# Another order of the 8 KB blocks of keys and values over the partitions

## The chip, the core and the metric

The kernel runs on one core of one Trainium2 chip. The time is device microseconds of one execution. The core has five engines: TensorE (PE, matrix products), VectorE (DVE), ScalarE (ACT), GpSimd (POOL) and SyncE (SP). Each has its own instruction stream, and they wait for one another with semaphores. On-chip memory (SBUF) has 128 partitions. Transfers between HBM and SBUF are carried by 16 DMA engines of the core; an instruction on SP's queue only starts a transfer.

## The reference

The program is the forward and backward pass of one decoding step: an attention block with cached keys and values beside a gated product of three weight matrices, both on a layer-normed row of 576 numbers, for a batch of 2. The gradients of all inputs but B_x are outputs, those of the caches too.

```python
q = (x @ wq).reshape(B, Sq, Hq, Dh).transpose(0, 2, 1, 3)   # 32 heads of 128, Sq = 1
k = jnp.repeat(k_cache, rep, axis=1)                        # 16 key heads, rep = 2
v = jnp.repeat(v_cache, rep, axis=1)
scores = jnp.einsum("bhqd,bhkd->bhqk", q, k) * (Dh ** -0.5) # 4096 keys
p = softmax(scores, axis=-1)
o = jnp.einsum("bhqk,bhkd->bhqd", p, v)
A = o.transpose(0, 2, 1, 3).reshape(B, Sq, Hq * Dh) @ wo
...
g = jnp.einsum("bsd,df->bsf", x, w_gate)
u = jnp.einsum("bsd,df->bsf", x, w_up)
Bo = jnp.einsum("bsf,fd->bsd", g * u, w_down)
...
return x + A + Bo                                           # and its vjp with grad_out
```

All data are bfloat16. One head of keys (or values) of one batch entry is 4096 rows of 128 numbers, 1 MiB. There are 32 such heads of keys and 32 of values, and 32 gradients of each kind to write.

## The kernel before

Everything is cut into 16 steps (s): a step is a group g of two key heads and one batch entry b. In a step two heads of keys and two of values are loaded, each into one tile `big` of 128 partitions x 4096 numbers. Partition p holds 32 keys in a row, the 8 KB block p of the 1 MiB. The keys are turned by VectorE (line 466, 32 x 32 blocks), scored against the queries on TensorE (`score`, line 1277), and go through a softmax over all keys of a head, in which maximum and sum run over partitions and free dimension alike. `dscore` does the same for values and the gradient of the output. `contract` (line 1451) sums values over keys with the weights, and keys over the score gradients, with the tiles as they were loaded. `head_outer` makes the gradient of one head of keys or values as an outer product (line 1299) into PSUM; ScalarE and VectorE copy it (lines 470 and 472) into another tile `big`, from which a store of 1 MiB writes it out. The same order of blocks holds in the loads, in all of the computation and in the stores.

Beside this run the weight matrices: their products with the rows, and their gradients, which are outer products too and are stored from tiles `big` and from two small tiles `tl` (the last 64 rows of a gradient, 64 KB).

The order of the instructions is settled before the launch. A planner (class `Order`) keeps a model of time, and generators yield what they want next: an engine for so long, a buffer, a wait, a transfer. It picks by start time and priority and so writes five fixed instruction streams. Nearly every transfer is started from SP: the loads of keys and values at line 1152 (`load_kv`), weights at lines 1171 to 1207 (`load_w`), and stores at line 699 (`put`). At most eight transfers of SP's queue are on the way at a time.

The names that matter below: `views` and `oviews` (lines 1140 and 1141) are the HBM arrays of the caches and of their gradients, cut so that an index of batch and head gives one head as partitions x numbers. `load_kv` takes `views`, and `head_outer` hands an item of `oviews` to `put` in line 1293. `tail_outer` stores the last 64 rows. For some of them, named by `few` (from `FEW_M` and `FEW_G`), it writes the HBM side with an outer dimension of 4, so that SBUF's 64 rows stand against 4 x 16 rows of HBM:

```python
dsts = [d.rearrange("(r q) f -> q r f", q=4) if k in few else d for k, d in enumerate(dsts)]
...
FEW_M, FEW_G = (NFS - 1,), range(3, NG)
```

With NFS = 9 and NG = 8, and `few=(0, 1) if i in FEW_M else (1,)` in the weight part, `few=(0,) if g in FEW_G else ()` in the attention part, these are 10 and 5 stores of 26.

Of the kernel before, what the change touches and what calls it, by code (L numbers as in the profile page):

```python
# [13 lines left out]
P = 128  # L14
# [340 lines left out]
def kernel(  # L355
# [781 lines left out]
    wS = [[None] * 2 for _ in range(NS)]  # L1137
    bE = [[Event() for _ in range(2)] for _ in range(NS)]
    bS = [[None] * 2 for _ in range(NS)]
    views = [A.rearrange("b h (p c) d -> b h p (c d)", p=P) for A in (A_k_cache, A_v_cache)]  # L1140
    oviews = [A.rearrange("b h (p c) d -> b h p (c d)", p=P) for A in (out_2, out_3)]

    def load_kv():
        n = 0
# [457 lines left out]
```

## Time and profile before

| | |
|---|---|
| median of 3 runs | 465.51 us (462.81 to 465.99) |
| the profiled execution's own time | 463.56 us |
| its span (first to last instruction) | 461.7 us |
| mean granted TensorE clock | 0.722 of full speed |
| bytes read from HBM, bytes written | 92.48 MB, 92.48 MB |

The page gives the busy time of each engine and its share of the span, then the span in 40 slices of 11.54 us: a digit is the busy share in tenths, and the row GB/s says what the DMA engines moved. A row of a DMA queue gives packets, megabytes and the time that the packets took, as a share of the time of all 16 DMA engines. The rows of DMA issues give what is moved, how many transfers and their size; SPq and ACTq are the queues that start them. The chain of waits is followed back from the last instruction: at each step to what released it. In rows of one source line, three numbers with slashes are the least, the median and the greatest time of an instruction in ns; for a DMA that is the time on the issuing queue, waiting included, not the transfer. DMA packets stand by size: "under 2 KB" includes those under 512 B, and so on.

### The profile page before, as it was taken

The page shows a single profiled execution, that of the slowest core. Times are in us where ns is not written, and L with a number is a line of the kernel's source. Part 1 is how long each engine was busy: PE and PEld are TensorE (multiplying, and loading weights), DVE is VectorE, ACT ScalarE, POOL GpSimd, SP SyncE. Part 2 cuts the span into 40 slices and gives each one's busy share as a digit, 9 for nine tenths or more (in the row PEclk, how much of TensorE's full clock was granted, in tenths as well). Part 3 has the DMA queues.
Part 4 walks back from the last instruction along what each step waited for, and adds up shares of the span by engine and source line. Part 5 has one row for each costly group of instructions (what it writes and reads, how often), then busy time and mean ns, then how long its engine had stood idle before and what let it go on. Part 6 is the DMA issues. An engine that isn't in the chain of part 4 may idle for free.

```text
span 461.7 us, 15711 instructions
## 1 busy us (share of the span) xinstructions
PE 365.6 (79%) x6750; PEld 210.9 (46%) x6750; DVE 365.9 (79%) x708; ACT 337.1 (73%) x516; POOL 143.1 (31%) x174
## 2 busy tenths in 40 slices
PE   1687879798987677897687787778988886887986
PEld 1444455556443343454455353544533543443453
DVE  8897888887789687869887688977867887877682
ACT  4268648778986596765857778858857997897873
POOL 0740044303407342560016251140344563053000
PEclk9969575966775677758975798956567685666855
DMA  8999999999999999999999999999999999999985
GB/s 316 414 410 421 412 426 397 416 416 387 357 424 424 407 424 410 422 419 413 411 405 419 418 421 420 424 412 412 409 422 425 415 422 424 422 389 393 423 310 202
DMA packets 40530, 185.97 MB, mean 403 GB/s; under 512 B 3460, under 2 KB 12172, under 8 KB 24076
## 3 DMA queue, kind: packets, MB, share of 16 engines
q1 hardware_dynamic: 40452, 184.96, 98.7%
q8 instruction: 53, 0.87, 0.7%
q14 instruction: 17, 0.14, 0.1%
q10 hardware_dynamic: 8, 0.00, 0.0%
HBM read 92.48 MB, written 92.48 MB: 401 GB/s over the span
## 4 chain that ended last, share of the span: by engine, by line
DMA 48%; PE 24%; DVE 14%; ACT 10%; issue 3%; POOL 1%; SPq 0%; ACTq 0%; DVEq 0%; POOLq 0%
DMA out_dram<-big 23%; DMA big<-in_A_v_cache_dram 15%; ACT big L470 8%; DVE big L466 7%; DMA big<-in_B_w_up_dram 6%; PE ps_o L1299 4%; PE ps_o L730 3%; PE ps_m L1277 3%; DMA big<-in_A_k_cache_dram 3%; PE ps_m L1451 3%; DVE big L472 2%; PE ps_m L895 1%; PE ps_m L681 1%; PE ps_o L767 1%; POOL BD L1265 1%
## 5 line engine op out<-in xcount | busy, mean ns | idle before, releaser
L470 ACT CAST big<-ps_o 128x1024 bf16<-128x1024 f32 (+2 forms) x309 | 278.8, 964 | 47.6 <-PE ps_o L1299 24.1
L466 DVE STREAM_TRANSPOSE big<-big 128x1024 f32<-128x1024 f32 x146 | 176.4, 1223 | 19.5 <-DMA big<-in_A_v_cache_dram 7.5
L1265 POOL TENSOR_TENSOR BD<-vr,mask 128x2048 bf16<-128x2048 bf16 x32 | 115.2, 3602 | 117.8 <-DVE vr L472 47.2
L472 DVE CAST big<-ps_o 128x1024 bf16<-128x1024 f32 (+1 forms) x69 | 73.3, 1064 | 17.4 <-PE ps_o L767 7.8
L1242 POOL COPY W<-rep 32x16 bf16<-32x16 bf16 x128 | 24.6, 192 | 116.5 <-DVE rep L1015 100.5
L1277 PE MATMUL ps_m<-big,W 128*32 128x128 bf16 x2048 | 58.1, 275 | 2.7 <-issue 1.0
L1277 PEld LDWEIGHTS <-W 128*32 128x32 bf16 x2048 | 46.2, 123 | 23.1 <-issue 21.8
L1299 PE MATMUL ps_o<-BD,dd 32*128 32x512 bf16 x256 | 46.6, 502 | 10.0 <-ACT big L470 7.8
L1299 PE MATMUL ps_o<-BD,pp 32*128 32x512 bf16 x256 | 44.5, 472 | 8.8 <-ACT big L470 7.0
L466 DVE STREAM_TRANSPOSE big<-ww 128x1152 f32<-128x1152 f32 (+1 forms) x25 | 33.0, 1319 | 4.1 <-DMA out_dram<-big 4.0
L1451 PE MATMUL ps_m<-big,pp 128*32 128x512 bf16 x256 | 28.9, 540 | 4.4 <-DVE pp L466 3.6
L1451 PE MATMUL ps_m<-big,dd 128*32 128x512 bf16 x256 | 28.5, 539 | 3.4 <-DVE dd L466 2.1
L1299 PEld LDWEIGHTS <-dd 32*128 32x128 bf16 x256 | 11.0, 98 | 26.9 <-issue 19.9
L1299 PEld LDWEIGHTS <-pp 32*128 32x128 bf16 x256 | 10.2, 96 | 28.7 <-issue 24.5
L767 PEld LDWEIGHTS <-xnr 32*128 32x128 bf16 x368 | 13.3, 116 | 14.6 <-issue 13.6
L767 PE MATMUL ps_o<-D,xnr 32*128 32x128 bf16 x256 | 14.0, 269 | 5.5 <-ACT big L470 3.8
L730 PE MATMUL ps_o<-dyr,R 32*32 32x288 bf16 x256 | 17.4, 391 | 1.2 <-ACT big L470 1.2
L1047 POOL COPY qr<-qd 128x256 bf16<-128x256 bf16 x8 | 3.2, 395 | 45.6 <-DVE qd L472 41.8
L730 PE MATMUL ps_o<-dyr,hb 32*32 32x288 bf16 x288 | 14.6, 313 | 2.2 <-ACT big L470 2.1
L1461 ACT ACTIVATE osb<-ps_m 128x512 bf16<-128x512 f32 x14 | 8.5, 604 | 9.9 <-PE ps_m L1451 9.9
L681 PE MATMUL ps_m<-big,wm 128*32 128x128 bf16 x416 | 13.1, 284 | 2.1 <-DVE cr L1403 1.2
L895 PE MATMUL ps_m<-big,Wdy 128*128 128x128 bf16 x162 | 14.0, 254 | 1.0 <-DVE oT L1471 0.6
(210 smaller groups left out, 487.4 us busy)
## 6 DMA issues: line engine op xcount, KB each, us to landing
out_dram<-big SPq DMA_DIRECT2D x74, 1024.0 KB
big<-in_A_k_cache_dram SPq DMA_DIRECT2D x32, 1024.0 KB
big<-in_A_v_cache_dram SPq DMA_DIRECT2D x32, 1024.0 KB
out_dram<-big SPq DMA_DIRECT2D x17, 576.0 KB
ww<-in_B_w_down_dram SPq DMA_DIRECT2D x9, 576.0 KB
ww<-in_A_wo_dram SPq DMA_DIRECT2D x8, 576.0 KB
ww<-in_A_wq_dram SPq DMA_DIRECT2D x8, 512.0 KB
big<-in_B_w_gate_dram SPq DMA_DIRECT2D x4, 1024.0 KB
```

The lines of the kernel that those rows point to most:

```text
L466: nc.vector.transpose(out, in_)
L470: nc.scalar.copy(out, in_)
L472: nc.vector.tensor_copy(out=out, in_=in_)
L681: nc.tensor.matmul(dp[32 * q:32 * q + 32, 0:P], lhsT=W, rhs=view(X, 0, P, xoff(q, s), [[FS, 4], [2, 32]]), start=(s == 0), stop=(s == S - 1))
L730: nc.tensor.matmul(o[32 * q:32 * q + 32, aa, 0:HD2], lhsT=view(t, 32 * q, 32, 2 * A + aa, [[4, 32]]), rhs=dyr[32 * q:32 * q + 32, k * HD2: ...
L767: nc.tensor.matmul(o[:, aa, j * P:(j + 1) * P], lhsT=xnr[32 * a:32 * a + 32, dc * P:(dc + 1) * P], rhs=rhs(a), start=True, stop=True)
L895: nc.tensor.matmul(dh, lhsT=Wdy[:, e, 2 * k:2 * k + P], rhs=view(X[:], 0, P, 64 * k + e, [[D, FC], [2, 32]]), start=(k == 0 and e == 0), s ...
L1242: nc.gpsimd.tensor_copy(view(W_t[t][w][:], 32 * a, 32, 6 + 8 * a, [[G * WW, 4], [WW, G], [1, 2]]), view(rep_t[grp[g]["qs"]][:], 32 * a, 32 ...
L1265: nc.gpsimd.tensor_tensor(BD_t[i][:], view(vr_t[v][:], 0, P, 0, [[0, 16], [1, Dh]]), view(mask16[:], 0, P, 0, [[1, 16], [0, Dh]]), ALU.mult)
L1277: nc.tensor.matmul(sc[32 * cq:32 * cq + 32, :], lhsT=view(W[:], 0, P, (be * G + l) * WW + 6 - 4 * c2 - 2 * l, [[1, 32]]), rhs=view(X[:], 0 ...
L1299: nc.tensor.matmul(o[:, k, :], lhsT=pr2[32 * c4:32 * c4 + 32, :], rhs=BD[32 * c4:32 * c4 + 32, 8 * l + 4 * h2:8 * l + 4 * h2 + 4, :], star ...
L1451: nc.tensor.matmul(ct[32 * j:32 * j + 32, :], lhsT=view(rT, 0, P, 4 * c + 2 * l, [[1, 32]]), rhs=kv_t[kvS[s][t][l]][:, Dh * c:Dh * (c + 4) ...
```

## The change

```diff
-    views = [A.rearrange("b h (p c) d -> b h p (c d)", p=P) for A in (A_k_cache, A_v_cache)]
-    oviews = [A.rearrange("b h (p c) d -> b h p (c d)", p=P) for A in (out_2, out_3)]
+    views, oviews = ([A.rearrange("b h (i j c) d -> b h j i (c d)", i=8, j=16) for A in As]
+                     for As in ((A_k_cache, A_v_cache), (out_2, out_3)))
```

One head is 128 blocks of 8 KB (32 keys). Before, partition p holds block p. After, the block number is written as 16i + j, with i from 0 to 7 and j from 0 to 15, and the HBM side of a transfer runs over j first, then i, then the block. So partition 8j + i holds block 16i + j: eight neighbouring partitions hold blocks that lie 16 blocks (128 KB) apart in HBM. The HBM side of these transfers now has three dimensions (16 x 8 x 4096 numbers) where it had two (128 x 4096); the SBUF side stays 128 partitions of 4096 numbers. Loads and stores both use the new order. Nothing else is edited.

## The prediction

> **What bounds the kernel now.** I read the page from the top: busy shares, the slices, the DMA queue, then the chain of waits.
>
> ```profile
> span 461.7 us, 15711 instructions
> PE 365.6 (79%) x6750; PEld 210.9 (46%) x6750; DVE 365.9 (79%) x708; ACT 337.1 (73%) x516; POOL 143.1 (31%) x174
> DMA  8999999999999999999999999999999999999985
> GB/s 316 414 410 421 412 426 397 416 416 387 357 424 424 407 424 410 422 419 413 411 405 419 418 421 420 424 412 412 409 422 425 415 422 424 422 389 393 423 310 202
> q1 hardware_dynamic: 40452, 184.96, 98.7%
> DMA 48%; PE 24%; DVE 14%; ACT 10%; issue 3%; POOL 1%; SPq 0%; ACTq 0%; DVEq 0%; POOLq 0%
> ```
>
> No compute engine is busy for more than 366 of 461.7 us, while the row of DMA digits stands at 9 from the second slice to the last but two. Queue q1, which carries everything that line 699 stores and lines 1152 to 1207 load, takes 98.7% of the time of all 16 DMA engines: 0.987 x 461.7 = 455.7 us of each. About 6 us are left, in the first slice and the last two. In the chain DMA has 48%; its compute links lie beside transfers that fill the engines anyway. So the bound is the time of the packets, and whatever lengthens or shortens a packet moves the end by nearly that much. The profiled execution took 463.56 us, 1.9 over its span, and stands 2 us under the median of 465.51; sums below are made on 463.6.
>
> **What is moved.** The whole-run view of the DMA queues counts the transfers.
>
> ```profile
> DMA packets 40530, 185.97 MB, mean 403 GB/s; under 512 B 3460, under 2 KB 12172, under 8 KB 24076
> out_dram<-big SPq DMA_DIRECT2D x74, 1024.0 KB
> big<-in_A_k_cache_dram SPq DMA_DIRECT2D x32, 1024.0 KB
> big<-in_A_v_cache_dram SPq DMA_DIRECT2D x32, 1024.0 KB
> out_dram<-big SPq DMA_DIRECT2D x17, 576.0 KB
> ww<-in_B_w_down_dram SPq DMA_DIRECT2D x9, 576.0 KB
> ww<-in_A_wo_dram SPq DMA_DIRECT2D x8, 576.0 KB
> ww<-in_A_wq_dram SPq DMA_DIRECT2D x8, 512.0 KB
> big<-in_B_w_gate_dram SPq DMA_DIRECT2D x4, 1024.0 KB
> big<-in_B_w_up_dram SPq DMA_DIRECT2D x4, 1024.0 KB
> out_dram<-tl SPq DMA_DIRECT2D x26, 64.0 KB
> out_dram<-big SPq DMA_DIRECT2D x2, 768.0 KB
> out_dram<-big SPq DMA_DIRECT2D x3, 512.0 KB
> big<-in_B_w_gate_dram SPq DMA_DIRECT2D x1, 512.0 KB
> big<-in_B_w_up_dram SPq DMA_DIRECT2D x1, 512.0 KB
> big<-in_B_w_gate_dram SPq DMA_DIRECT2D x1, 448.0 KB
> big<-in_B_w_up_dram SPq DMA_DIRECT2D x1, 448.0 KB
> tq<-in_A_wq_dram SPq DMA_DIRECT2D x1, 384.0 KB
> tq<-in_A_wq_dram SPq DMA_DIRECT2D x1, 128.0 KB
> gu<-in_B_w_gate_dram SPq DMA_DIRECT2D x1, 128.0 KB
> gu<-in_B_w_up_dram SPq DMA_DIRECT2D x1, 128.0 KB
> out_dram<-xy SPq DMA_DIRECT2D x2, 2.2 KB
> xy<-in_A_x_dram ACTq DMA_DIRECT2D x1, 2.2 KB
> xy<-in_grad_out_dram ACTq DMA_DIRECT2D x1, 2.2 KB
> ```
>
> The change touches the 64 loads of keys and values and, of the 74 big stores, the 64 that line 1293 hands to line 699. These are 128 x 1.0486 MB = 134.2 MB of the 185.97.
>
> The same rows show how a transfer is dealt to engines. 227 transfers are on SP's queue without the four of xy. The smallest packets, under 512 B, close a transfer on each engine that took part. If all 227 had used 16 engines and xy's four, of two rows, two each, there would be 227 x 16 + 4 x 2 = 3640. There are 3460, or 180 fewer, and 180 = 15 x 12: fifteen transfers ran on 4 engines only. Fifteen is the number of tail stores that the code writes with an outer dimension of 4 on the HBM side (FEW_M and FEW_G: 10 and 5). So the slowest dimension of the two sides sets the split, and an outer 64 or 128 goes to 16. After the change the HBM side's outer dimension is j with 16 values: still 16 engines, still eight packets of 8 KB each, and engine j gets partitions 8j to 8j+7.
>
> **The change part by part.**
>
> Packets, bytes and instructions: the order of instructions of the changed kernel is the same on all five engines, and only the address patterns of those 128 transfers differ. Compute sees other keys in a partition, but a softmax and a sum over keys don't depend on it, and stores use the same map as loads. Cost 0, with nothing that has to hide it.
>
> Issue: the address pattern gets one more dimension. The nearest rows are a two-dimensional and a three-dimensional load:
>
> ```profile
> L1152 SPq DMA_DIRECT2D big<-in_A_k_cache_dram x32: 327/438/5976, 0.7 to 389.3; - x32
> L1174 SPq DMA_DIRECT2D ww<-in_A_wq_dram x8: 385/751/1209, 1.6 to 322.7; - x8
> ```
>
> The shortest issues (first of the three numbers, ns) differ by 58 ns, which over 128 transfers is 7.4 us on SP. The full DMA engines hide it: the next transfer waits in the queue meanwhile. With the cover gone it would cost up to 7.4 us; I take 0.
>
> HBM side: an engine now steps 128 KB from packet to packet, and the 16 engines side by side read one stretch of 128 KB. No row has this pattern, so I bound it. The stretch from 338 to 351 us is nearly all keys, values and their gradients:
>
> ```profile
> core 0 of [0], span 461.7 us
> DMA packets 760, 5.55 MB, mean 427 GB/s; under 512 B 84, under 2 KB 84, under 8 KB 84
> ```
>
> At 427 GB/s the 134.2 MB take 314 us, 157 for each direction. That is the best rate of these long stretches, so a better address order could at most lift the other slices to it. The 37 full slices average 413; at 427 they would take 37 x 11.54 x 14 / 427 = 14 us less, and by bytes 134.2 / 185.97 = 72% of it, 10 us, could belong to the changed transfers. The slower slices also hold many small packets, so I take 0 and keep -10 as an end.
>
> SBUF side: this is the part that decides. Before, nearly every transfer cuts the same 128 rows in the same way, so each engine serves the same eight partitions all the time, and whatever ways lead into SBUF, no two engines have to share one. After it, 128 of 231 transfers are cut otherwise, in runs of eight neighbouring partitions. If the ways belong to the old groups, two engines meet on one. The lower end is nothing: the ways are not full, or the groups are the same. At the upper end two engines in step share one way all the time, and every changed packet takes twice as long: +314 us, or +157 if only loads suffer. Between these, take two engines whose runs of four packets on one way (length L alone) are shifted by d. Sharing equally, they need 2L - d for the run: 1.5 L if any shift is as likely, 2 L in step. I take 1.6, a little above the mean, since all engines are handed a transfer together.
>
> For stores one row speaks against it:
>
> ```profile
> DMA packets 528, 2.28 MB, mean 415 GB/s; under 512 B 62, under 2 KB 190, under 8 KB 365
> q1 hardware_dynamic: 527, 2.26, 100.3%
> ```
>
> This is 50.5 to 56 us. 190 - 62 = 128 packets of 1 KB are two tail stores from 64 partitions, which cut SBUF in another way than the full stores around them, and the rate stays at 415. A burst of 64 KB is short, but nothing was lost. So I charge loads alone: 157 x 0.6 = 94 us. Sum: 463.6 + 94 = 558, say **560 us**.
>
> The Trainium skill states what the trace cannot show. In "SBUF — State Buffer", section "Door 1: The DMA port swizzle", partitions p and p + 32 lie on one of 16 ports, each worth some 27 GB/s, and a load into 64 partitions was measured at 196 GB/s against 328 into 128. In "DMA: Bandwidth & Descriptors", section "The descriptor swizzle", a 128-partition transfer gives every engine one port of its own, two groups of four partitions. By these, engines j and j + 4 would meet on the same two ports after the change, stores as well as loads, and in step the sum would be 464 + 314 = 778; the tail stores' row does not agree for stores, and no run here shows it for loads.
>
> **The rivals.**
>
> Both directions share: as above with 314 x 0.6 = 188, giving 652, and up to 778 in step. For it: loads and stores get the same map. It is what the port map of the Trainium skill ("SBUF — State Buffer", the section named above) would do here. Against it: the tail stores' row. Chance 0.20.
>
> No effect, the other side: the SBUF ways carry two engines, or the queue regroups the rows as before, and the packets keep their rate. Place: every changed packet; price 0; it decides as soon as one way passes two packets of 8 KB in the time of one, about 0.31 us (16 x 13 us / 676 packets of 338 to 351 us). For it: packet time goes by size at every pattern that the kernel has, and the slices never fall far. Time 464, between 462 and 467. Chance 0.29.
>
> A better HBM order with no sharing: part of the 10 us comes off, 453 to 459. Against it: 427 GB/s is held in long stretches already. Chance 0.07.
>
> A small loss, from address order or issue, with SBUF not shared: the 7.4 us of issue, or a few per cent of 314, so 469 to 500. Chance 0.08.
>
> **How the numbers follow.** Loads sharing ways, 560 us, has 0.36 and is the likeliest single case; its own range goes from a factor 1.4 (463.6 + 63 = 526) to 2 (621). The range has to hold the case of no effect as well, so it starts at 462. It ends at 665, just over the middle of the two-way case. Left out are the gain (0.07) and the upper part of the two-way case (about 0.10). Within 1%, some 4.6 us and about what a measurement can tell from no change, lies the case of no effect: 0.29. Faster is 0.07, slower 0.36 + 0.20 + 0.08 = 0.64.
>
> **What would show it.** The queue's row must keep its packets and bytes; its share should stay near 98% of a longer span, or the engines are waiting, not slow. Right if in stretches of loads the rate falls well under 427 GB/s (to about 270 at the factor 1.6) while stretches of stores stay near 415. If both fall, the two-way rival holds. If the slices stand at 410 to 425 and the span is near 462, ways are not shared, and the step of the SBUF side is wrong. Compute busy times should not grow, but for the granted clock. If the number of small packets changes, the split over engines is not what I read from it.

## The result and the profile after

The changed kernel takes 564.79 us (median of 4, 559.29 to 565.86) against 465.75 (462.81 to 466.1): the ratio is 1.212, with a 95% interval of 1.203 to 1.221. It is slower by 99 us. Ratios leave disturbed runs out; for the kernel with new loads alone, below, that leaves the two lower ones of four.

These are lines of the changed kernel's page: span and busy times, the DMA digits and GB/s of the 40 slices (now 14.08 us each), the packets, and SP's queue.

```profile
span 563.0 us, 15711 instructions
PE 387.5 (69%) x6750; PEld 222.5 (40%) x6750; DVE 367.8 (65%) x708; ACT 339.1 (60%) x516; POOL 143.1 (25%) x174
DMA  8999999999999999999999999999999999999985
GB/s 223 229 310 298 287 391 306 386 318 363 361 376 355 262 287 360 287 351 346 346 256 349 234 396 356 332 378 357 329 365 387 344 360 380 398 367 330 416 274 167
DMA packets 40530, 185.97 MB, mean 330 GB/s; under 512 B 3460, under 2 KB 12172, under 8 KB 24076
q1 hardware_dynamic: 40452, 184.96, 98.7%
```

Packets, bytes and the small packets that tell the number of engines are the same to the last one, and the share of q1 is again 98.7%. So the engines do not wait for work; each packet occupies its engine longer, and the 101.3 us that the span has gained are DMA time. The packet records of the two traces (start, size and time of every packet) tell whose packets these are. The 16384 packets of 8 KB on SP's queue are those of the 128 edited transfers: 0.315 us each before, 0.392 after, 79 us more for each of the 16 engines. The packets of all other transfers take another 21 us, though nothing was edited in them. VectorE and ScalarE are busy as long as before (within 2 us); TensorE is up by 22 us at a lower mean clock (0.676 against 0.722), but has work for only 69% of the span. Where the time goes is seen in the first two slices: 223 and 229 GB/s, where the kernel before had 316 and 414. They hold nothing but loads, of keys, values and weights. Later slices, with loads and stores mixed, swing between 234 and 416, but for the last one.

### The profile page after: what moved, and what is told of

Read it like the earlier page. It is cut to its first block, busy times and chain, and to the rows that moved or that the text cites. A ratio compares the mean times of both kernels' runs of the same rounds, so it can differ in the third digit from the quotient of the medians.

```text
span 563.0 us, 15711 instructions
## 1 busy us (share of the span) xinstructions
PE 387.5 (69%) x6750; PEld 222.5 (40%) x6750; DVE 367.8 (65%) x708; ACT 339.1 (60%) x516; POOL 143.1 (25%) x174
## 2 busy tenths in 40 slices
DMA packets 40530, 185.97 MB, mean 330 GB/s; under 512 B 3460, under 2 KB 12172, under 8 KB 24076
## 3 DMA queue, kind: packets, MB, share of 16 engines
q1 hardware_dynamic: 40452, 184.96, 98.7%
## 5 line engine op out<-in xcount | busy, mean ns | idle before, releaser
L1277 PE MATMUL ps_m<-big,W 128*32 128x128 bf16 x2048 | 62.6, 289 | 5.6 <-issue 4.2
L1277 PEld LDWEIGHTS <-W 128*32 128x32 bf16 x2048 | 49.6, 129 | 28.3 <-issue 27.2
L1299 PE MATMUL ps_o<-BD,pp 32*128 32x512 bf16 x256 | 48.1, 519 | 12.2 <-DVE big L472 5.4
L1299 PE MATMUL ps_o<-BD,dd 32*128 32x512 bf16 x256 | 48.1, 531 | 9.4 <-ACT big L470 4.9
L1451 PE MATMUL ps_m<-big,pp 128*32 128x512 bf16 x256 | 31.6, 578 | 14.1 <-DVE pp L466 12.6
L1352 ACT COPY mr<-m 1x128 f32<-1x128 f32 x16 | 4.7, 296 | 33.3 <-DVE m L1350 33.3
L1299 PEld LDWEIGHTS <-dd 32*128 32x128 bf16 x256 | 10.8, 101 | 25.5 <-issue 17.6
L730 PE MATMUL ps_o<-dyr,R 32*32 32x288 bf16 x256 | 18.7, 415 | 2.6 <-ACT big L470 2.6
L877 PE MATMUL ps_m<-big,xs 128*32 128x128 bf16 x344 | 11.1, 289 | 9.7 <-DMA big<-in_B_w_up_dram 5.4
L895 PE MATMUL ps_m<-big,Wdy 128*128 128x128 bf16 x162 | 16.1, 277 | 1.5 <-DVE oT L1471 0.9
```

Source lines behind the costliest of these rows:

```text
L730: nc.tensor.matmul(o[32 * q:32 * q + 32, aa, 0:HD2], lhsT=view(t, 32 * q, 32, 2 * A + aa, [[4, 32]]), rhs=dyr[32 * q:32 * q + 32, k * HD2: ...
L877: nc.tensor.matmul(ug[32 * a:32 * a + 32, 1 - w, :], lhsT=xs[:, k, :], rhs=rhs, start=(dc == 0), stop=(dc == 4))
L895: nc.tensor.matmul(dh, lhsT=Wdy[:, e, 2 * k:2 * k + P], rhs=view(X[:], 0, P, 64 * k + e, [[D, FC], [2, 32]]), start=(k == 0 and e == 0), s ...
L1277: nc.tensor.matmul(sc[32 * cq:32 * cq + 32, :], lhsT=view(W[:], 0, P, (be * G + l) * WW + 6 - 4 * c2 - 2 * l, [[1, 32]]), rhs=view(X[:], 0 ...
L1299: nc.tensor.matmul(o[:, k, :], lhsT=pr2[32 * c4:32 * c4 + 32, :], rhs=BD[32 * c4:32 * c4 + 32, 8 * l + 4 * h2:8 * l + 4 * h2 + 4, :], star ...
L1451: nc.tensor.matmul(ct[32 * j:32 * j + 32, :], lhsT=view(rT, 0, P, 4 * c + 2 * l, [[1, 32]]), rhs=kv_t[kvS[s][t][l]][:, Dh * c:Dh * (c + 4) ...
```

## The experiments

**Loads alone, stores alone.** In the first kernel only the loads have the new order, in the second only the stores. This is the edit of the first against the changed kernel; the second has the two orders the other way round:

```diff
-    views, oviews = ([A.rearrange("b h (i j c) d -> b h j i (c d)", i=8, j=16) for A in As]
-                     for As in ((A_k_cache, A_v_cache), (out_2, out_3)))
+    views = [A.rearrange("b h (i j c) d -> b h j i (c d)", i=8, j=16) for A in (A_k_cache, A_v_cache)]
+    oviews = [A.rearrange("b h (p c) d -> b h p (c d)", p=P) for A in (out_2, out_3)]
```

> Loads of keys and values in the new order, stores in the old one (so the rows of the two gradients lie in other places of the outputs). Theory, engines meet on a way into SBUF and only loads suffer: all of the loss stays, 555 to 570 us. Rival, both directions suffer alike: about half of the 99 us, 505 to 525. Rival, the order of addresses in HBM costs, in both directions: also about half.

> Stores in the new order, loads in the old one (gradient rows again in other places). Theory, only loads suffer: no loss, 462 to 468 us. Rival, both directions: 505 to 525 us.

Loads alone: ratio 1.1905 (1.1849 to 1.1961) to the 464.08 us of the kernel before on that chip, or +88 us. That is some 552 us, just under the 555 to 570 that were expected. Its four runs spread from 551.0 to 565.8; the median, 557.93, would give +94. Stores alone: ratio 1.0615 (1.0565 to 1.0666), +28 us. Loads make the larger part, as expected. But stores are not free, and not half of the loss either: neither the theory nor the rival had that. And 88 + 28 = 116 is more than the 99 of both together, so the two parts overlap.

**The order of addresses in HBM.** Two more orders of the same kernel, in loads and stores alike. This is the edit of the first against the changed kernel; the second has `i=4, j=32` in both new lines:

```diff
-    views, oviews = ([A.rearrange("b h (i j c) d -> b h j i (c d)", i=8, j=16) for A in As]
-                     for As in ((A_k_cache, A_v_cache), (out_2, out_3)))
+    views = [A.rearrange("b h (i j c) d -> b h j i (c d)", i=2, j=64) for A in (A_k_cache, A_v_cache)]
+    oviews = [A.rearrange("b h (i j c) d -> b h j i (c d)", i=2, j=64) for A in (out_2, out_3)]
```

> Another order: partition 2j+i holds block 64i+j, j from 0 to 63. An engine still gets eight neighbouring partitions, but reads two stretches of 32 KB where it now reads eight blocks 128 KB apart, and the 16 engines do not read one common stretch. Theory, the SBUF groups cost: 540 to 575 us. Rival, the 128 KB steps or the common stretch in HBM cost: 462 to 475 us.

> The changed kernel with i from 0 to 3 and j from 0 to 31 instead of 0 to 7 and 0 to 15: partition 4j+i holds block 32i+j, in loads and stores. HBM side as scattered as in the change (steps of 256 KB for one engine, engines side by side). Theory, groups of four partitions must stay on one engine: 462 to 468 us. Rival, the order in HBM costs: 540 to 575 us.

The first took 465.23 us, ratio 1.002 (1.0006 to 1.0034); the second 464.86, ratio 1.0001 (0.998 to 1.0023). So the loss is gone in both. For 64 x 2 that spoke against my theory at first: I had taken it that any outer dimension which is a multiple of 16 leaves an engine eight neighbours. It left two readings: either HBM addresses were the cost, or the queue keeps groups of four neighbouring partitions whole where the outer dimension lets it (64 x 2: two values of j make a group; 32 x 4: one; 16 x 8: half a one). The 32 x 4 order decides it. There HBM is as scattered as in the change, with steps of 256 KB for an engine and the engines side by side, and the time is that of the kernel before. This is its GB/s row, 300 in the first slice and 414 in the second:

```profile
GB/s 300 414 407 424 391 417 395 413 408 378 352 415 424 407 423 395 417 416 408 415 403 415 418 412 421 422 417 412 395 416 408 419 422 422 425 412 379 422 362 206
```

**The transfers by themselves.** The first probe leaves out all computation: it runs nine stages of 16 transfers, and VectorE writes into every tile between stages, so that the queue runs dry there. This and the three probes below ran once each; their code is given in short form.

```python
load_old:   big[h % 8][:]        <- A_k_cache[0, h] as 128 x 4096
load_new:   big[h % 8][:]        <- A_k_cache[0, h] as 16 x 8 x 4096 (the change)
load_near:  big[h % 8][:]        <- A_k_cache[0, h] as 64 x 2 x 4096
load_low:   big[h % 8][0:64, :]  <- half a head as 64 x 4096
load_mid:   big[h % 8][32:96, :] <- half a head as 64 x 4096
store_old, store_new, store_low, store_mid: the same ways outward, without 64 x 2
```

> No computation at all, only nine stages of 16 transfers each with nothing else on the queue; outputs are not computed. Theory, loads alone share ways into SBUF (GB/s in the middle of a stage): loads of 128 partitions in the old order 415 to 430; in the new order 205 to 270; with 64 x 2 blocks 205 to 270; loads into partitions 0 to 63 about 213, into 32 to 95 about 420, if a way belongs to partitions p and p+32 and not to those 64 apart; all four kinds of stores 410 to 430. Rival, both directions share: stores in the new order and from partitions 0 to 63 fall to 205 to 270 too. Rival, HBM order costs: loads into partitions 0 to 63 keep 410 or more, and the 64 x 2 order is faster than the new one.

From the DMA view of the probe, one window in the middle of each stage, in the order of the stages: loads old, new, 64 x 2, partitions 0 to 63, 32 to 95; stores old, new, 0 to 63, 32 to 95.

```profile
DMA packets 1159, 8.45 MB, mean 422 GB/s; under 512 B 128, under 2 KB 128, under 8 KB 128
...
DMA packets 1195, 8.74 MB, mean 219 GB/s; under 512 B 128, under 2 KB 128, under 8 KB 128
...
DMA packets 1162, 8.47 MB, mean 424 GB/s; under 512 B 128, under 2 KB 128, under 8 KB 128
...
DMA packets 629, 4.13 MB, mean 206 GB/s; under 512 B 125, under 2 KB 125, under 8 KB 125
...
DMA packets 841, 5.51 MB, mean 424 GB/s; under 512 B 168, under 2 KB 168, under 8 KB 168
...
DMA packets 1152, 8.39 MB, mean 419 GB/s; under 512 B 128, under 2 KB 128, under 8 KB 128
...
DMA packets 1161, 8.46 MB, mean 423 GB/s; under 512 B 128, under 2 KB 128, under 8 KB 128
...
DMA packets 638, 4.18 MB, mean 209 GB/s; under 512 B 128, under 2 KB 128, under 8 KB 128
...
DMA packets 768, 4.99 MB, mean 416 GB/s; under 512 B 159, under 2 KB 159, under 8 KB 159
```

Loads in the new order move at half the rate, 219 against 422. Partitions 0 to 63 halve the rate too, in both directions, while just as many partitions from 32 to 95 do not. That agrees with the Trainium skill, "SBUF — State Buffer", section "Door 1: The DMA port swizzle", which puts p and p + 32 on one port and p + 64 on another; its 196 GB/s for a load into 64 partitions stands beside 206 here. So stores do share ways, against my theory. Yet stores in the new order run at 423 in mid-stage. The GB/s row of that whole stage (274 to 319.5 us, 40 slices of 1.1 us) tells why:

```profile
GB/s 0 230 223 245 281 375 382 403 418 411 439 403 432 439 418 411 439 411 418 432 411 447 411 425 439 411 418 432 389 447 432 403 425 432 396 439 425 266 86 7
```

It starts at half the rate and is above 400 after some 7 us. The packet records show the same for single packets: 8 KB take 0.61 us on the mean in the middle of the stage of new loads, and 0.31 in the middle of the stage of new stores, as in the old order. A reading that fits, though the trace names no engine and so doesn't show it: two engines that share two ways, four packets on each, need not wait if one is four packets behind the other, and stores come into that position by themselves. Loads in this order did not: their stage, 16.8 MB at 219 GB/s, lasts some 77 us.

**Addresses against groups, and mixed traffic.** The second probe first loads with the groups of the change but other addresses (each engine 64 KB in one piece, 72 KB from the next), then in the 32 x 4 order, and then has 16 loads and 16 stores in turn: both old, new loads, new stores, both new.

```python
load_spaced: big[h % 8][:] <- 16 rows 9 * 4096 numbers apart, 8 x 4096 numbers from each
load_fours:  big[h % 8][:] <- A_k_cache[0, h] as 32 x 4 x 4096
for h in range(16): load(h); store(h)        # four times, with old and new
```

> Again no computation, six stages. First, loads whose HBM side is 16 runs of eight blocks one behind another, the runs 72 KB apart (16 x 8 x 4096, data of no use): an engine reads 64 KB in one piece, no two engines near one another. Theory, eight neighbouring partitions to an engine is the cost: 205 to 220 GB/s. Rival, the order in HBM: 415 to 430. Second, loads in the order 32 x 4 (partition 4j+i holds block 32i+j): steps of 256 KB, engines side by side in HBM as in the changed kernel, but groups of four partitions stay whole. Theory: 415 to 430. Rival, order in HBM: 205 to 300. Then loads and stores in turn, 16 of each: both old 400 to 425; new loads with old stores 300 to 390, since an engine's twin is in a store half of the time; old loads with new stores 380 to 425, since in the first probe stores alone came out of step in some 8 us and then kept 423; both new not above new loads with old stores.

Its DMA view: a window within the first stage, one within the second, and then the four mixed stages whole. The last line is the GB/s row of the stage with new loads and old stores.

```profile
DMA packets 1255, 9.10 MB, mean 228 GB/s; under 512 B 144, under 2 KB 144, under 8 KB 144
...
DMA packets 1396, 10.15 MB, mean 423 GB/s; under 512 B 157, under 2 KB 157, under 8 KB 157
...
DMA packets 4610, 33.57 MB, mean 399 GB/s; under 512 B 512, under 2 KB 512, under 8 KB 512
...
DMA packets 4608, 33.56 MB, mean 321 GB/s; under 512 B 512, under 2 KB 512, under 8 KB 512
...
DMA packets 4608, 33.56 MB, mean 392 GB/s; under 512 B 512, under 2 KB 512, under 8 KB 512
...
DMA packets 4608, 33.56 MB, mean 315 GB/s; under 512 B 512, under 2 KB 512, under 8 KB 512
...
GB/s 245 220 430 223 292 361 220 367 295 245 421 239 317 383 239 361 352 270 414 311 308 399 276 374 314 283 405 317 370 380 364 411 380 430 424 427 427 270 88 9
```

228 against 423: addresses without the groups cost nothing, groups with plain addresses cost the half. The mixed stages give the price with no kernel around them. 33.56 MB at 321 instead of 399 GB/s are 104.5 - 84.1 = 20.4 us for 16 loads, so 82 us for 64; the kernel with new loads had 88. The last row swings between 220 and 430, and the swing grows smaller. That fits loads in step and stores in turn, with partners that drift apart, but which transfer runs when is not in the row. For 16 new stores the same sum gives 85.6 - 84.1 = 1.5, or 6 us for 64, where the kernel lost 28.

**Why stores cost more in the kernel.** The third probe puts old and new stores through what the kernel does to them: small stores on four engines between them, weight loads of 128 x 2304 between them, and a dry queue before every fourth. A seventh stage tries to set engines 0 to 3 behind by four packets.

```python
for h in range(16): store(h); store_tail(h)          # stages 1 (old), 2 (new)
for h in range(16): store(h); load_weight(h)         # stages 3, 4
for h in range(16):                                  # stages 5, 6
    if h % 4 == 0: between()
    store(h)
load_four_engines(); for h in range(16): load_new(h) # stage 7
```

> Why stores in the new order cost the kernel 28 us when the second probe has both kinds in turn almost free: seven stages of transfers, no computation. One: 16 old stores, each followed by a 64 KB store on four engines; two: the same with new stores; three: 16 old stores, each followed by a weight load of 128 x 2304 numbers; four: the same with new stores; five: 16 old stores in four bursts with the queue run dry before each; six: the same with new stores; seven: one load of 512 KB on four engines (engines 0 to 3 fall four packets behind), then 16 new loads. Theory A, a dry queue puts the engines back in step: stage six 10 to 16 us longer than five, two and four within 4 us of one and three. Theory B, four-engine transfers do it: two 10 us or more longer than one. Theory C, other groups of partitions in between do it: four 10 us or more longer than three. Seven: if engines 0 to 3 meet engines 4 to 7, they now pass each other and only eight engines still wait, so the DMA share falls from 101% to some 75%, at 205 to 230 GB/s as before, since a load is complete only with its slowest engine. If partners are neighbours (0 with 1), nothing changes and the share stays at 101%.

The load of the seventh stage was 128 KB, not the 512 that I wrote: four packets for each of four engines, as was meant. From the DMA view: the stages one to four whole, then one burst of stage five and one of stage six, and the GB/s row of that last burst (13.7 us); then a window within stage seven and its share of the engines.

```profile
DMA packets 3392, 17.83 MB, mean 328 GB/s; under 512 B 320, under 2 KB 1344, under 8 KB 1344
...
DMA packets 3392, 17.84 MB, mean 301 GB/s; under 512 B 319, under 2 KB 1343, under 8 KB 1343
...
DMA packets 4608, 26.22 MB, mean 397 GB/s; under 512 B 512, under 2 KB 512, under 8 KB 2560
...
DMA packets 4608, 26.22 MB, mean 350 GB/s; under 512 B 512, under 2 KB 512, under 8 KB 2560
...
DMA packets 576, 4.19 MB, mean 407 GB/s; under 512 B 64, under 2 KB 64, under 8 KB 64
...
DMA packets 576, 4.19 MB, mean 306 GB/s; under 512 B 64, under 2 KB 64, under 8 KB 64
...
GB/s 359 167 239 167 239 215 144 215 383 359 287 167 335 383 383 335 359 383 407 383 454 407 383 407 407 431 383 431 455 454 431 431 359 287 263 191 72 48 48 0
...
DMA packets 1877, 13.67 MB, mean 228 GB/s; under 512 B 209, under 2 KB 209, under 8 KB 209
...
q1 hardware_dynamic: 1877, 13.67, 101.6%
```

Megabytes by rate give the times. A dry queue costs 13.7 - 10.3 = 3.4 us a burst, 14 us for the four, as theory A has it, and the GB/s row shows a restart at half the rate. The other bursts of the two stages take as long within 0.3 us. But theory A also wanted the other two pairs of stages within 4 us, and they are not: four-engine stores cost 59.3 - 54.4 = 5 us, weight loads 74.9 - 66.0 = 9 us. Theory B, 10 us or more for four-engine stores, falls. Theory C is just short of the 10 that I had asked of it, and the first restart accounts for some 3.4 of the 9.

A dry queue is not what costs the kernel its 28 us. These are lines of the page of the kernel with new stores alone:

```profile
DMA  8999999999999999999999999999999999999993
GB/s 322 409 415 398 354 376 400 397 338 351 421 394 339 373 381 390 400 389 416 376 354 403 365 388 379 404 377 353 376 407 379 417 414 399 403 383 384 406 280 125
q1 hardware_dynamic: 40452, 184.96, 97.9%
```

The engines stay busy from the second slice to the last but one; in the packet records, from 12 to 475 us, fewer than eight packets run at once for 0.1 us in all. Instead the rate is lower through most of the kernel.

Weight loads in between fit that in size. In mid-stage, away from the restart, stage three moves 422 GB/s (160 to 195 us) and stage four 374 (225 to 270 us). A store with its weight load is 1.64 MB, so new stores cost 1.64 / 0.374 - 1.64 / 0.422 = 0.50 us each, and in the kernel 28 / 64 = 0.44. That weight loads are cut in the old way is not enough for it: in the second probe, loads in the old order between new stores left 424 GB/s in mid-stage (325 to 385 us). Weight loads differ from those in their packets, 4.6 KB instead of 8 KB. Whether that is what disturbs the offset was not tried, and which transfers do it in the kernel was not traced.

Stage seven changed nothing (101.6%). By what I had written, that speaks for neighbours as partners, which the fourth probe refutes. I take it to tell nothing: a transfer ends with its slowest engine, and eight at most are on the way, so engines that run ahead may soon have empty queues and start the next one in step again. That was not tried.

**Which partitions share a way.** The fourth probe uses few engines: 16 rows on 16 engines into partitions 0 to 15, the same on four engines, 64 rows on four engines into 0 to 63, and into 32 to 95.

```python
big[h % 8][0:16, :]  <- 16 x 4096                # one row an engine
big[h % 8][0:16, :]  <- 4 x 4 x 4096             # four engines, four rows each
big[h % 8][0:64, :]  <- 4 x 16 x 4096            # four engines, 16 rows each
big[h % 8][32:96, :] <- 4 x 16 x 4096
```

> Which partitions share a way: four stages of 16 loads each, rows of 8 KB, no computation. Theory: a way serves four neighbours p and the four at p+32, whatever engines use it, at 427 / 16 = 26.7 GB/s. One, 16 rows on 16 engines into partitions 0 to 15 (four ways): about 107 GB/s although 16 engines work. Two, the same 16 rows on four engines, four rows each (one way for each engine): about 107 too. Three, 64 rows on four engines into partitions 0 to 63 (engines 0 and 2, and 1 and 3, go through the same ways in step): about 53. Four, 64 rows on four engines into partitions 32 to 95 (no two meet): about 107. Rival, the engines are what is short and not the ways: one gives 400 or more, two, three and four about 107. Rival, neighbouring groups share: two falls to 53.

From its DMA view, a window in each of the stages one, two and four, with the share of the 16 engines for the first two, and for stage three the GB/s row of the whole stage (85.5 us).

```profile
DMA packets 349, 1.43 MB, mean 110 GB/s; under 512 B 175, under 2 KB 175, under 8 KB 175
...
q1 hardware_dynamic: 349, 1.43, 103.6%
...
DMA packets 260, 1.70 MB, mean 107 GB/s; under 512 B 52, under 2 KB 52, under 8 KB 52
...
q1 hardware_dynamic: 260, 1.70, 25.5%
...
DMA packets 828, 6.39 MB, mean 106 GB/s; under 512 B 48, under 2 KB 48, under 8 KB 48
...
GB/s 61 65 65 77 73 84 96 100 103 107 107 103 107 107 107 103 107 107 107 107 107 103 103 107 107 107 107 107 103 107 107 107 107 103 107 107 107 107 77 34
```

Sixteen engines, all marked busy (103.6%), move no more than four engines at 25.5%, and by the packet records 8 KB take 1.20 us in the first stage and 0.31 in the second: what is short is the way, 107 / 4 = 27 GB/s each. Four engines on four neighbouring groups do not meet. In the third stage they meet at first (61 GB/s; 53 was expected) and come out of step within some 20 us, so loads can do that too. The mean of that stage, 98, lies near what no sharing would give, and only its row shows what happened.

## Why the prediction was right

*The bound.* Right: q1's share is 98.7% before and after, and the lengthening of the packets went into the end undiminished.

*How a transfer is dealt to engines.* Right for the change (3460 small packets in both), but too coarse. That the outer dimension is a multiple of 16 is not the whole condition: 32 x 4 and 64 x 2 lose nothing, 16 x 8 does. The runs fit groups of four partitions that stay whole in the first two. The trace names no engine, so the dealing itself is inferred.

*HBM side, taken as 0.* Right: 32 x 4 is at 1.0001, and the spaced loads of the second probe lose half with plain addresses. The gain of up to 10 us isn't there in either order.

*SBUF side, loads: 157 x 0.6 = 94 us.* Right in kind and nearly in size: +88 in the kernel (+94 by the median of its four runs), 82 by the second probe. The factor 1.6 was a guess between 1.5 and 2, and 1.52 to 1.60 come out of these; alone, loads are near 2 (422 against 219 GB/s). In stretches of loads I had named a sign of about 270 GB/s; the first two slices have 223 and 229. The prediction also lengthened the edited packets alone, while 21 us of the longer packet time lie in transfers that were not edited. That these meet the edited ones on a way would explain it, but was not tried.

*SBUF side, stores: 0.* Wrong: +28 us. The step that failed is the reading of the two tail stores in the window from 50.5 to 56 us as a sign that stores lose nothing on shared ways. They do: the first probe has stores from 64 partitions at 209 GB/s when they are alone. The window could not show it. In the packet records its 128 packets of 1 KB start over two microseconds, from 51.9 to 54.0, and take 0.046 us each, the median of all packets of that size. That fits engines that came to these stores at different moments and were done with a burst of 64 KB before they could meet. The rival with both directions had the sharing right; its price of 188 us or more was wrong, because it took a share of waiting that stores do not keep (423 GB/s in mid-stage).

*The sum.* 558 against a measured 564.8. It came out close partly by luck, because errors cancel: stores were left out (28 us), and loads and stores overlap (88 + 28 against 99). Why they overlap was not tried; one reading is that partners held apart by one direction stay apart in the other. The second probe has no such overlap: both new cost 106.5 - 84.1 = 22.4 us, against 20.4 + 1.5. The range, 462 to 665, reached from no effect into the two-way case, so that lying within it says little; the single case that I chose had 0.36.

*Issue, up to 7.4 us, hidden.* Hidden indeed, but the size was off. The line of key loads in the changed kernel, with the least time first:

```profile
L1152 SPq DMA_DIRECT2D big<-in_A_k_cache_dram x32: 536/595/6274, 0.7 to 481.7; - x32
```

536 - 327 = 209 ns more each, not 58, and stores in the first probe have 537 against 332; over 128 transfers that is 27 us of SP. The 32 x 4 kernel has the same pattern of dimensions and lost nothing.

## What to carry to other kernels

When a kernel is bound by its DMA engines, check of every reordering of a transfer whether each engine still goes to its own partitions of SBUF: packets, bytes and busy share stayed the same here when it did not, and only GB/s and the time of a packet told. Here, 128 partitions as 128, 64 x 2 or 32 x 4 on the HBM side kept the full rate, and 16 x 8 halved that of loads. If HBM needs blocks dealt in turn, keep four neighbouring partitions together.

## What the runs showed of the hardware that was not expected

- Stores in the 16 x 8 order begin at some 225 GB/s and are above 400 after some 7 us; loads in the same order stayed near 219 for a stage of some 77 us. Why loads stay in step is open: stage three of the fourth probe shows that loads of four engines do come out of it, from 61 to 107 GB/s.
- A dry queue puts partners back in step: 3.4 us for each restart of four stores in that order.
- Old-order loads with packets of 8 KB between such stores cost next to nothing (424 GB/s against 427 with both old, in mid-stage), weight loads with packets of 4.6 KB cost 0.50 us a store. Why is open.
- A DMA engine that waits for a way counts as busy: 16 engines at 103.6% moved 110 GB/s, with 1.20 us for a packet of 8 KB.
- Starting a load of 8 KB rows whose HBM side has three dimensions took SP at least 536 ns in the changed kernel, with two 327 in the kernel before.
